# Part 2's first layer as Strassen's seven quarter products in place of eight

## The chip, the cores and the metric

The kernel runs on one core of one Trainium2 chip. The metric is the device time of one execution in microseconds, as the median of a few runs. The core has five engines that take their own instruction streams and wait for one another through semaphores: TensorE (PE, with its weight loads listed apart as PEld), VectorE (DVE), ScalarE (ACT), GpSimd (POOL) and SyncE (SP), which here only issues transfers.

## The reference

```python
scores = q @ mean_of_8(k).T / sqrt(64)          # per batch 8, head 8; 576 x 72
x = softmax(scores) @ mean_of_8(v)              # -> 4608 tokens x 512
h = max(x @ w1, x @ w2, x @ w3)                 # 512 -> 768
x = h @ w_out                                   # 768 -> 512
h = max(x @ moe2_w_in, 0)                       # 512 -> 2048   (first layer of part 2)
out = (h * h) @ moe2_w_out                      # 2048 -> 512   (second layer of part 2)
```

The feed-forward weights are 64-bit floats, which the kernel is handed as raw bits; q, k, v and the result (4608 x 512) are float32.

## The kernel before

Every product is done in three TensorE passes over values that are split into a high and a low part (`PARTS`: high x high, high x low, low x high); `split` makes the parts, the high one on ACT by a copy that rounds, the low one by a subtraction on DVE or POOL.

Part 1 works on 12 blocks of 384 tokens (`T1`). A block is 22 steps: 18 products of the max layer (L404, 12 matmuls of 384 columns each) and 4 of its output layer (L422, 18 matmuls each), whose results `ys` go to `y_dram` in DRAM by transfers on ACT's queue (L429). The attention of block j + 1 is woven between the steps of block j. So is, from block 2 to block 10, the preparation of part 2's weights: the 64-bit rows of `wi2` and `wo2` are loaded into a raw buffer (L118, two buffers for them in this stretch), turned into float32 by ACT and DVE (L133 to L138, result `wbits`), split in place (L115, L116, the low part on POOL), and stored to `wi2_dram` and `wo2_dram` (L386). `todo` is a list of pieces with due times, sorted once and emitted in that order. Behind it stands the planner of the framework, which emits on each engine the earliest piece in program order that it believes to be ready; a pool opened after others were closed takes their memory, and each of its tiles waits for the old tiles under it.

Part 2 works on 9 blocks of 512 tokens (`T2`). A block is 16 steps; in step f `moe2_in` multiplies a 128-column slice of the first layer's weights with the block (L505, 12 matmuls of 512 columns into one of three PSUM banks `ps`), ACT and DVE make the squared positive part and its two parts `g` (L511 to L515), and two steps later (`LAG`) `moe2_out` adds it into four PSUM banks `acc` (L526, 12 matmuls of 512 columns). All weights of part 2 stay in SBUF after they have been fetched once (L471): ten tiles of 512 KB during part 1's last block, 22 when part 1's memory comes free. `load_y` (L477) fetches and splits the next block's tokens.

SBUF from the bottom in part 1, by the pools' sizes per partition: `w_p` 96 KB (six `spare` tiles first, then 18 tiles of the max layer), `x_p` 24 KB, `h_p` 18 KB, `t_p` 6 KB (`hm`, then `ys`).

Of the kernel before, what the change touches and what calls it, by code (L numbers as in the profile page):

```python
# [10 lines left out]
F32 = mybir.dt.float32  # L11
F32R = mybir.dt.float32r
# [8 lines left out]
P = 128  # L21
# [5 lines left out]
DM = H * D  # L27
# [45 lines left out]
def as_f32(ap):  # L73
    return ap.bitcast(F32)
# [3 lines left out]
def attention_moe_kernel(ctx: ExitStack, tc: tile.TileContext, q, k, v, vn, w1, w2, w3, wo1, wi2, wo2, out):  # L78
# [18 lines left out]
    wi2_dram = [dram.tile([P, 2, 512], F32, name=f"wi2_dram{f}") for f in range(KF2)]  # L97
# [14 lines left out]

    def split(hl, src, engine=nc.vector):

        nc.scalar.activation(hl[:, 0], src, AF.Copy)  # L115
        engine.tensor_tensor(out=hl[:, 1], in0=src, in1=as_f32(hl[:, 0]), op=ALU.subtract)  # L116

    def load_raw(raw_pool, src):  # L118
# [4 lines left out]
    def convert(pool, raw_pool, raw, name, tag=None):  # L123

        low, high = raw[:, :, 0], raw[:, :, 1]
        a = raw_pool.tile([P, 512], I32, tag="row", name="wbits")
# [8 lines left out]
        if pool is None:  # L141
            w = raw.rearrange("p a b -> p (a b)").rearrange("p (c a) -> p c a", c=2).bitcast(F32R)
        else:
            w = pool.tile([P, 2, 512], F32R, name=name, tag=tag or name)
        split(w, as_f32(a), nc.gpsimd)
        return w
# [132 lines left out]

    def attend(j, b, s0, n, p, t):  # L280
# [4 lines left out]
        def load():  # L285
            if j == 0:
                kq = early([P, 2 * 512], "kq")
                kr.append(kq[:, :S])
                qr.append(kq[:, S : S + n])
                nc.sync.dma_start(out=kr[0], in_=k[b, p])  # L290
            elif first:
                kr.append(load_k(b, p))
            if j:
                qr.append(raw_p.tile([P, 512], F32, tag="row", name="qr")[:, :n])
# [10 lines left out]
        def softmax(tiles):  # L305
# [6 lines left out]
            ss = sm_p.tile([P, 3, 2, SP], F32, tag="ss", name="ss")[:m, :g]  # L312
# [66 lines left out]
    def load_w1(f, e):  # L379
        w1_t[f, e] = convert(w_p, raw_p, load_raw(raw_p, (w1, w2, w3)[e][f]), f"w1_{f}_{e}")  # L380

    def load_second(src, raw):
        raw.append(load_raw(raw_p, src))

    def prepare_second(raw, dst, name):
        nc.sync.dma_start(out=dst, in_=as_f32(convert(None, raw_p, raw.pop(), name)))  # L386

    def load_wo1(kk):
        wo1_t[kk] = convert(w_p, raw_p, load_raw(raw_p, wo1[kk]), f"wo1_{kk}", spare[kk])
        shared[0] = kk < KF1 - 1  # L390

    def moe1(j):
# [3 lines left out]
        for f in range(KF1):  # L396
# [19 lines left out]
            hs.append(h)  # L416
        for d in range(KD):
# [12 lines left out]
            yield  # L430
# [22 lines left out]
    for f in range(KF2):  # L453
        second += [(wi2[f], wi2_dram[f], f"wi2_{f}"), (wo2[f], wo2_dram[f], f"wo2_{f}")]
    for i, (src, dst, name) in enumerate(second):
        when, raw = STEPS * (SECOND[0] + (i + 0.5) * (SECOND[1] - SECOND[0]) / len(second)), []
        todo.append((when - LEAD_SECOND, functools.partial(load_second, src, raw)))
        todo.append((when, functools.partial(prepare_second, raw, dst, name)))
# [3 lines left out]

    y_p = ctx.enter_context(tc.tile_pool(name="y_p", bufs=1, side="right", reuse_waits="tile"))
    w2_p = ctx.enter_context(tc.tile_pool(name="w2_p", bufs=1, side="right", reuse_waits="tile"))
    wi2_t, wo2_t, y_t = {}, {}, {}
    NR = 10

    def fetch_second(t, f, pool):
        name, src = ("wi2", wi2_dram) if t is wi2_t else ("wo2", wo2_dram)
        t[f] = pool.tile([P, 2, 512], F32R, name=f"{name}s_{f}")  # L470
        nc.sync.dma_start(out=as_f32(t[f]), in_=src[f])  # L471


    order = sorted([(f, 0, wi2_t) for f in range(KF2)] + [(f + LAG, 1, wo2_t) for f in range(KF2)], key=lambda a: a[:2])
    loads = [(n, functools.partial(fetch_second, t, n - LAG if t is wo2_t else n)) for n, _, t in order]

    def load_y(j, d, pool):  # L477
        yr = y_p.tile([P, T2], F32, tag="yr", name="yr", bufs=2)
        t = 0
        while t < T2:  # L480
            i, o = divmod(j * T2 + t, T1)
            n = min(T2 - t, T1 - o)
            nc.sync.dma_start(out=yr[:, t : t + n], in_=y_dram[i][d, :, o : o + n])
            t += n
        y_t[j, d] = pool.tile([P, 2, T2], F32R, tag=f"y{d}", name=f"y{d}")
        split(y_t[j, d], yr)
# [7 lines left out]
    s1.close()  # L494
    w3_p = ctx.enter_context(tc.tile_pool(name="w3_p", bufs=1, reuse_waits="tile"))
    y2_p = ctx.enter_context(tc.tile_pool(name="y2_p", bufs=1, reuse_waits="tile"))
    g_p = ctx.enter_context(tc.tile_pool(name="g_p", bufs=3, reuse_waits="tile"))
    acc_ps = ctx.enter_context(tc.tile_pool(name="acc_ps", bufs=1, space=PSUM, reuse_waits="tile"))

    def moe2_in(j, f):  # L500
        ps = mm_ps.tile([P, T2], F32, tag="ps", name="ps")
        n = 0
        for kk in range(KD):
            for a, c in PARTS:
                nc.tensor.matmul(  # L505
                    ps, lhsT=wi2_t[f][:, a, kk * P : (kk + 1) * P], rhs=y_t[j, kk][:, c],
                    start=(n == 0), stop=(n == 3 * KD - 1),
                )
                n += 1
        r = g_p.tile([P, T2], F32, tag="r", name="r", bufs=2)  # L510
        nc.scalar.activation(r, ps, AF.Relu)  # L511
        g = g_p.tile([P, 2, T2], F32R, tag="g", name="g")
        nc.scalar.activation(g[:, 0], r, AF.Square)  # L513
        nc.vector.tensor_tensor(out=r, in0=r, in1=r, op=ALU.mult)  # L514
        nc.vector.tensor_tensor(out=g[:, 1], in0=r, in1=as_f32(g[:, 0]), op=ALU.subtract)  # L515
        return g

    NTT = T2 // P
    acc_t = {}

    def moe2_out(j, f, g):
        if f == 0:
            acc_t[j] = [acc_ps.tile([P, DM], F32, tag=f"acc{i}", name=f"acc{i}") for i in range(NTT)]
        for i in range(NTT):
            for n, (a, c) in enumerate(PARTS):
                nc.tensor.matmul(  # L526
                    acc_t[j][i], lhsT=g[:, a, i * P : (i + 1) * P], rhs=wo2_t[f][:, c],
                    start=(f == 0 and n == 0), stop=(f == KF2 - 1 and n == 2),
                )
            if f == KF2 - 1:  # L530
                o = g_p.tile([P, DM], F32, tag="o", name="o", bufs=4)
# [7 lines left out]
    late = [(n - AHEAD, functools.partial(f, w3_p)) for n, f in loads[NR:]]  # L539
    steps = [(j, f) for j in range(NB2) for f in range(KF2)]  # L540
    gs = {}
    for n, (j, f) in enumerate(steps):
        while late and late[0][0] <= n:
            late.pop(0)[1]()
        if f % 2 and f // 2 < KD and j + 1 < NB2:
            load_y(j + 1, f // 2, y2_p if j % 2 == 0 else y_p)
        gs[n] = moe2_in(j, f)
        if n >= LAG:
            moe2_out(*steps[n - LAG], gs.pop(n - LAG))
    for n in range(len(steps) - LAG, len(steps)):  # L550
        moe2_out(*steps[n], gs.pop(n))
# [41 lines left out]
```

## Time and profile before

| | |
|---|---|
| median of 3 runs | 1587.5 us (1587.31 to 1587.64) |
| profiled execution | 1590.31 us, span 1588.6 us |
| mean granted TensorE clock | 0.981 |
| PE busy | 1554.8 us (98%) |
| DVE, ACT, POOL busy | 748.9, 665.9, 174.1 us |
| HBM read, written | 83.89, 35.65 MB |

The span is the time from the first to the last instruction of the program; the profiled execution's own time lies 1.7 us above it. Matmul records overlap (one runs on while the next has begun), so the mean ns of one matmul is longer than the distance from one to the next; the latter is the length of a stretch over the matmuls in it.

### The profile page before, as it was taken

To read this page: it belongs to the slowest core of one execution; us is meant where nothing else is said; L and a number is where in the kernel's file an instruction comes from. 1 tells how busy PE (TensorE), PEld (TensorE's weight loads), DVE (VectorE), ACT (ScalarE), POOL (GpSimd) and SP (SyncE) were. 2 spreads that over 40 slices of the span, in tenths; PEclk is the share of its full clock that TensorE was granted. 3 is DMA by queue.
4 is the path that set the end of the run, shared out by engine and by line. 5 is a ranking of instruction groups with operands and counts; after the bars stand their busy time and mean duration, and the time that the engine had idled before them with its cause. 6 is when DMAs were issued, how large, how long until landed. Compare 5 with 4: busy or idle time off the path is not lost.

```text
span 1588.6 us, 21815 instructions
## 1 busy us (share of the span) xinstructions
PE 1554.8 (98%) x7994; PEld 1387.3 (87%) x7994; DVE 748.9 (47%) x1644; ACT 665.9 (42%) x1837; POOL 174.1 (11%) x223
## 2 busy tenths in 40 slices
PE   7889999999998999999999999999999999999998
PEld 5789999999998999999988888888888888888886
DVE  6896667675686657753233323232323223232222
ACT  7775556655566556653122223232322223232221
POOL 5541112222122102210000000000000000000000
PEclk7799999999999999999999999999999999999999
DMA  5552224432244214404270101010100001010000
GB/s 194 176 183 87 82 74 160 135 114 70 90 143 144 97 46 131 150 30 153 78 286 12 42 1 53 0 54 1 53 1 27 27 1 53 1 40 1 27 0 27
DMA packets 56652, 120.96 MB, mean 76 GB/s; under 512 B 6337, under 2 KB 29889, under 8 KB 56545
## 3 DMA queue, kind: packets, MB, share of 16 engines
q1 hardware_dynamic: 49632, 110.12, 20.8%
q10 hardware_dynamic: 6912, 9.44, 1.6%
q8 instruction: 63, 1.03, 0.3%
q14 instruction: 45, 0.36, 0.1%
HBM read 83.89 MB, written 35.65 MB: 75 GB/s over the span
## 4 chain that ended last, share of the span: by engine, by line
PE 89%; DMA 3%; DVE 3%; ACT 2%; issue 1%; POOL 1%; DVEq 0%; SPq 0%; ACTq 0%; POOLq 0%
PE ps L404 25%; PE ps L505 25%; PE acc L526 25%; PE ps L422 8%; PE sc L317 2%; PE tr L343 2%; PE av L369 1%; PE av L368 1%; DMA wraw<-in_w_dram 1%; DVE wbits L135 1%; ACT ss L322 1%; DMA wi_dram<-wraw 0%; DMA wraw<-in_wi_dram 0%; DVE wbits L138 0%; ACT wbits L133 0%
## 5 line engine op out<-in xcount | busy, mean ns | idle before, releaser
L404 PE MATMUL ps<-x,w 128*128 128x384 f32 x2592 | 505.6, 343 | 5.9 <-DVE hm L412 3.3
L404 PEld LDWEIGHTS ps<-x,w 128*128 128x128 f32 x2592 | 451.3, 191 | 9.5 <-DVE hm L412 4.1
L505 PE MATMUL ps<-y,wi2s 128*128 128x512 f32 x1728 | 420.6, 391 | 0.0
L526 PE MATMUL acc<-wo2s,g 128*128 128x512 f32 x1728 | 420.1, 391 | 0.0
L526 PEld LDWEIGHTS acc<-wo2s,g 128*128 128x128 f32 x1728 | 324.5, 188 | 71.5
L505 PEld LDWEIGHTS ps<-y,wi2s 128*128 128x128 f32 x1728 | 324.4, 188 | 71.5
L514 DVE TENSOR_TENSOR r<-r 128x512 f32<-128x512 f32 x144 | 99.5, 691 | 491.2 <-ACT g L513 491.2
L511 ACT ACTIVATE r<-ps 128x512 f32<-128x512 f32 x144 | 86.1, 598 | 546.6 <-PE ps L505 540.0
L422 PE MATMUL ps<-h,wo 128*128 128x384 f32 x864 | 166.8, 342 | 1.5 <-DVE hm L412 1.5
L422 PEld LDWEIGHTS ps<-h,wo 128*128 128x128 f32 x864 | 151.6, 191 | 1.7 <-DVE hm L412 1.7
L328 POOL TENSOR_TENSOR ss<-ss,st 128x144 f32<-128x144 f32 (+3 forms) x144 | 84.8, 589 | 438.7 <-DVE st L327 244.3
L412 DVE TENSOR_TENSOR hm<-ps,hm 128x384 f32<-128x384 f32 x144 | 79.5, 552 | 68.3 <-PE ps L404 63.1
L515 DVE TENSOR_TENSOR g<-r,g 128x512 fp32r<-128x512 f32 x144 | 99.5, 691 | 13.5 <-DVE r L514 0.9
L322 ACT ACTIVATE ss<-sc,st 128x72 f32<-128x72 f32 (+1 forms) x320 | 98.4, 314 | 12.4 <-DVE st L319 10.8
L345 ACT ACTIVATE pt<-tr 72x256 fp32r<-72x256 f32 (+1 forms) x160 | 56.4, 356 | 92.0 <-PE tr L343 90.0
L346 DVE TENSOR_TENSOR pt<-tr,pt 72x256 fp32r<-72x256 f32 (+1 forms) x160 | 62.0, 389 | 69.4 <-ACT pt L345 68.4
L513 ACT ACTIVATE g<-r 128x512 fp32r<-128x512 f32 x144 | 90.9, 632 | 4.3
L317 PE MATMUL sc<-kbd,qs 128*128 128x144 f32 (+1 forms) x480 | 79.1, 278 | 8.4 <-ACT kbd L177 5.5
L317 PEld LDWEIGHTS sc<-kbd,qs 128*128 128x128 f32 (+1 forms) x480 | 74.7, 197 | 12.5 <-issue 6.2
L343 PE MATMUL tr<-ident,ss 128*72 128x128 f32 (+1 forms) x320 | 60.5, 275 | 8.7 <-DVE pt L346 8.4
L322 ACT ACTIVATION_READ_ACCUMULATOR ss<-sc,st 128x1 f32 (+1 forms) x320 | 63.6, 199 | 0.0
L319 DVE TENSOR_REDUCE st<-sc 128x2 f32<-128x144 f32 (+3 forms) x144 | 45.4, 315 | 37.5 <-PE sc L317 37.0
(60 smaller groups left out, 1036.6 us busy)
## 6 DMA issues: line engine op xcount, KB each, us to landing
wraw<-in_wo_dram SPq DMA_DIRECT2D x22, 512.0 KB
wraw<-in_w_dram SPq DMA_DIRECT2D x18, 512.0 KB
y_dram<-ys ACTq DMA_DIRECT2D x48, 192.0 KB
out_dram<-o SPq DMA_DIRECT2D x36, 256.0 KB
wraw<-in_wi_dram SPq DMA_DIRECT2D x16, 512.0 KB
wi_dram<-wraw SPq DMA_DIRECT2D x16, 512.0 KB
wo_dram<-wraw SPq DMA_DIRECT2D x16, 512.0 KB
wi2s<-wi_dram SPq DMA_DIRECT2D x16, 512.0 KB
```

The source lines that it names most:

```text
L317: nc.tensor.matmul(src[:, i], lhsT=lhsT, rhs=kbd[:, p, l], start=(n == 0), stop=(n == 2))
L322: nc.scalar.activation(ss[:, i, h], src[:, i, h], AF.Exp, bias=st[:, 0, i, h : h + 1], accum_out=st[:, 1, i, h : h + 1],)
L328: nc.gpsimd.tensor_tensor(out=ss, in0=ss, in1=st[:, 2].rearrange("p g (h o) -> p g h o", o=1).to_broadcast([m, g, 2, SP]), op=ALU.mult,)
L343: nc.tensor.transpose(tr[:, h, :m], sms[c][:, h], ident[:m, :m])
L404: nc.tensor.matmul(ps, lhsT=w1_t[f, e][:, a, kk * P : (kk + 1) * P], rhs=x[kk][:, c], start=(n == 0), stop=(n == 3 * KD - 1),)
L422: nc.tensor.matmul(ps, lhsT=wo1_t[kk][:, a, d * P : (d + 1) * P], rhs=hs[kk][:, c], start=(n == 0), stop=(n == 3 * KF1 - 1),)
L505: nc.tensor.matmul(ps, lhsT=wi2_t[f][:, a, kk * P : (kk + 1) * P], rhs=y_t[j, kk][:, c], start=(n == 0), stop=(n == 3 * KD - 1),)
L511: nc.scalar.activation(r, ps, AF.Relu)
L513: nc.scalar.activation(g[:, 0], r, AF.Square)
L514: nc.vector.tensor_tensor(out=r, in0=r, in1=r, op=ALU.mult)
L515: nc.vector.tensor_tensor(out=g[:, 1], in0=r, in1=as_f32(g[:, 0]), op=ALU.subtract)
L526: nc.tensor.matmul(acc_t[j][i], lhsT=g[:, a, i * P : (i + 1) * P], rhs=wo2_t[f][:, c], start=(f == 0 and n == 0), stop=(f == KF2 - 1 and n ...
```

## The change

The first layer of part 2 takes two weight slices from each half of the hidden width and two halves (256 tokens, `HT`) of a block as a 2 x 2 by 2 x 2 product of quarters and does it in seven quarter products (the Winograd form of Strassen's scheme). A group (`gr`, four to a block) covers four slices of 128. `product` does two slices (u) of one of the seven products into one bank, in 2 x 6 matmuls of 256 columns. `moe2_in` adds the seven up on DVE. `mix_y` makes the four token combinations, `split_y` splits the seven operands. The weights' combinations are made in part 1 (`prepare_in`), per pair of rows: four stored tiles of 512, 512, 512 and 256 columns (`WIDTHS`). The first layer's weights stay in SBUF (14 KB per pair and partition, 8 pairs); the second layer's are fetched for every group of every block (`fetch_group`, four tiles of 512 KB, five buffers). `moe2_out` follows in the same group, in four phases of 12 matmuls of 512 columns. In part 1 the loads and conversions are tied by one-element copies on POOL to the latest `hm` of the max layer; `row` buffers go from four, shared with `qr`, to three and two of its own; three score tiles share an `ss` buffer.

```diff
+    def load_raw(raw_pool, src, after=None):
         raw = raw_pool.tile([P, 512, 2], I32, tag=place(0), name="wraw", bufs=1)
+        if after is not None:
+            nc.gpsimd.tensor_copy(as_f32(raw[:1, 0, :1]), after[:1, :1])
         nc.sync.dma_start(out=raw.rearrange("p a b -> p (a b)"), in_=src.bitcast(I32))
...
+    def prepare_in(raw, rows, f):
+        rows.append(convert(raw_p, raw[0], now[0]))
+        if f % 2 == 0:
+            split(in_place(raw[0]), rows[0], nc.gpsimd)
+            store_second(wi2_dram[f // 2][0], in_place(raw[0]))
+            return
...
+        combine(c[:, l], a2[:, l], a2[:, r], ALU.add)
+        combine(c[:, r], c[:, l], a1[:, l], ALU.subtract)
+        combine(a2[:, l], a1[:, l], a2[:, l], ALU.subtract)
+        combine(a1[:, r], a1[:, r], c[:, r], ALU.subtract)
+        split(in_place(raw[0]), a2, nc.gpsimd)
+        store_second(dst[1], in_place(raw[0]))
+        hi, lo = a2.bitcast(F32R), c.bitcast(F32R)
+        split_to(hi, lo, c, nc.gpsimd)
+        store_second(dst[2][:, 0], hi)
+        store_second(dst[2][:, 1], lo)
+        hi, lo = a1[:, l].bitcast(F32R), a1[:, r].bitcast(F32R)
+        split_to(hi, lo, a1[:, r], nc.gpsimd)
+        store_second(dst[3].rearrange("p a b -> p (a b)"), a1)
...
+    g_p = ctx.enter_context(tc.tile_pool(name="g_p", bufs=5, reuse_waits="tile"))
+    s_p = ctx.enter_context(tc.tile_pool(name="s_p", bufs=1, reuse_waits="tile"))
     w3_p = ctx.enter_context(tc.tile_pool(name="w3_p", bufs=1, reuse_waits="tile"))
+    wo_p = ctx.enter_context(tc.tile_pool(name="wo_p", bufs=5, reuse_waits="tile"))
...
+    def product(j, gr, m):
+        bank = mm_ps.tile([P, T2], F32, tag="ps", name="ps")
+        i, o = PLACES[m]
+        for u in range(2):
+            n = 0
+            for kk in range(2):
+                for a, c in PARTS:
+                    nc.tensor.matmul(
+                        bank[:, u * HT : (u + 1) * HT],
+                        lhsT=wi2_t[2 * gr + u][i][:, a, o + kk * P : o + (kk + 1) * P],
+                        rhs=y_t[j][m][:, c, kk], start=(n == 0), stop=(n == 5),
+                    )
+                    n += 1
+        return bank
+
+    def squared(c):
+        g = g_p.tile([P, 2, T2], F32R, tag="g", name="g")
+        nc.vector.scalar_tensor_tensor(out=c, in0=c, scalar=0.0, in1=c, op0=ALU.max, op1=ALU.mult)
+        split(g, c)
+        return g
+
+    def total(name, bank, other):
+        c = s_p.tile([P, T2], F32, tag=name, name=name)
+        nc.vector.tensor_tensor(out=c, in0=bank, in1=other, op=ALU.add)
+        return c
+
+    def moe2_in(j, gr):
+        m1 = product(j, gr, 1)
+        s1 = s_p.tile([P, T2], F32, tag="s1", name="s1")
+        nc.scalar.activation(s1, m1, AF.Copy)
+        s2 = total("s2", product(j, gr, 6), s1)
+        s3 = total("s3", product(j, gr, 7), s2)
+        m5 = product(j, gr, 5)
+        g = {(1, 1): squared(total("c0", m5, s3))}
+        nc.vector.tensor_tensor(out=s2, in0=m5, in1=s2, op=ALU.add)
+        g[0, 0] = squared(total("c1", product(j, gr, 2), s1))
+        g[1, 0] = squared(total("c0", product(j, gr, 4), s3))
+        g[0, 1] = squared(total("c1", product(j, gr, 3), s2))
+        return g
...
+    for p in range(1, NP2):
+        fetch_in(p, w3_p)
+        if p == 1:
+            fetch_group(0, 0)
+    for j in range(NB2):
+        for gr in range(NG):
+            if gr == 0 and j + 1 < NB2:
+                for r in range(2):
+                    load_y(j + 1, r)
+            g = moe2_in(j, gr)
+            if gr == NG - 2 and j + 1 < NB2:
+                mix_y(j + 1)
+            if gr == NG - 1 and j + 1 < NB2:
+                for m in ORDER:
+                    split_y(j + 1, m)
+            for h, half in ((1, 1), (0, 0), (1, 0), (0, 1)):
+                moe2_out(j, gr, h, half, g[h, half])
+            nxt = j * NG + gr + 1
+            if nxt < NB2 * NG:
+                fetch_group(*divmod(nxt, NG))
```

## Rows read from the trace of the kernel before

**Rows 1.** The page: busy us (share) x instructions of each engine.
```profile
PE 1554.8 (98%) x7994; PEld 1387.3 (87%) x7994; DVE 748.9 (47%) x1644; ACT 665.9 (42%) x1837; POOL 174.1 (11%) x223
```

**Rows 2.** Busy time by stage: us, each engine (instructions), clock, DMA share, GB/s.
```profile
140.00:300.00 160.00, 159.70 (x995) 157.38 (x994) 110.75 (x294) 93.79 (x312) 29.16 (x43) 1.00 0.32 102
...
450.00:600.00 150.00, 145.73 (x883) 142.22 (x883) 99.43 (x264) 87.70 (x289) 27.80 (x41) 0.98 0.30 101
...
788.00:1588.60 800.60, 795.11 (x3475) 651.70 (x3473) 231.61 (x338) 207.52 (x340) 0.00 (x0) 1.00 0.11 37
```

**Rows 3.** Groups of instructions: count | busy us, mean ns | idle before.
```profile
L505 PE MATMUL ps<-y,wi2s 128*128 128x512 f32 x1728 | 420.6, 391 | 0.0
L526 PE MATMUL acc<-wo2s,g 128*128 128x512 f32 x1728 | 420.1, 391 | 0.0
...
L505 PEld LDWEIGHTS ps<-y,wi2s 128*128 128x128 f32 x1728 | 324.4, 188 | 71.5
```

**Rows 4.** Windows of PE alone: 384-column stretch, then 512-column stretch.
```profile
745.00:785.00 40.00, 40.00 (x233) 1.00 0.27 100
...
1100.00:1500.00 400.00, 400.00 (x1749) 1.00 0.06 20
```

**Rows 5.** Timeline of PEld near 85 us: start, us, loads of 128 columns.
```profile
85.59 0.74 PEld L358 LDWEIGHTS av<-pt,vst 72*128 72x128 f32 x6
```

**Rows 6.** Groups of ACT, DVE, POOL by form: x count | busy us, mean ns.
```profile
L514 DVE TENSOR_TENSOR r<-r 128x512 f32<-128x512 f32 x144 | 99.5, 691 | 491.2 <-ACT g L513 491.2
L513 ACT ACTIVATE g<-r 128x512 fp32r<-128x512 f32 x144 | 90.9, 632 | 4.3
L533 DVE COPY o<-acc 128x512 f32<-128x512 f32 x18 | 12.3, 691 | 38.1 <-PE acc L526 37.5
L346 DVE TENSOR_TENSOR pt<-tr,pt 72x256 fp32r<-72x256 f32 x96 | 40.0, 416 | 46.2 <-ACT pt L345 45.5
L116 POOL TENSOR_TENSOR wraw<-wbits,wraw 128x512 fp32r<-128x512 f32 x32 | 41.2, 1287 | 61.6 <-ACT wraw L115 54.3 <-issue 3.8 <-DVE st L327 3.4
```

**Rows 7.** Timeline of DVE in a quiet part-2 step.
```profile
993.02 0.69 DVE L514 TENSOR_TENSOR r<-r 128x512 f32<-128x512 f32 x1 [3.98 <-ACT g L513]
993.81 0.69 DVE L515 TENSOR_TENSOR g<-r,g 128x512 fp32r<-128x512 f32 x1
```

**Rows 8.** Timeline where the next block's tokens are split.
```profile
960.15 0.69 DVE L514 TENSOR_TENSOR r<-r 128x512 f32<-128x512 f32 x1 [1.30 <-ACT g L513]
...
961.39 0.69 DVE L116 TENSOR_TENSOR y<-yr,y 128x512 fp32r<-128x512 f32 x1 [0.55 <-ACT y L115]
962.00 0.68 DVE L515 TENSOR_TENSOR g<-r,g 128x512 fp32r<-128x512 f32 x1
```

**Rows 9.** Timeline of the passage from part 1 to part 2.
```profile
788.57 0.32 SPq L471 DMA_DIRECT2D wi2s<-wi_dram  x1
...
790.98 8.55 PE L505 MATMUL ps<-y,wi2s 128*128 128x512 f32 x37
...
791.70 0.33 ACTq L429 DMA_DIRECT2D y_dram<-ys  x1
```

**Rows 10.** Windows around that passage, columns as in rows 2.
```profile
755.00:788.00 33.00, 33.00 (x192) 33.00 (x191) 7.13 (x13) 5.05 (x10) 0.00 (x0) 1.00 0.11 39
788.00:800.00 12.00, 12.00 (x59) 10.47 (x58) 4.06 (x6) 5.11 (x10) 0.00 (x0) 1.00 0.89 335
800.00:818.00 18.00, 18.00 (x80) 14.83 (x80) 5.86 (x9) 5.22 (x9) 0.00 (x0) 1.00 1.03 405
```

**Rows 11.** The chain that ended last, 485 to 492 us: start, us, what.
```profile
485.17 3.53 DMA wi_dram<-wraw
488.72 3.03 DMA wraw<-in_wi_dram
```

**Rows 12.** Windows behind it, columns as in rows 2.
```profile
494.00:506.00 12.00, 7.73 (x44) 6.33 (x43) 10.48 (x29) 9.07 (x34) 2.80 (x4) 0.90 0.44 145
506.00:513.00 7.00, 7.00 (x32) 6.83 (x32) 5.20 (x18) 4.63 (x15) 3.13 (x4) 0.68 0.27 104
```

More of the change, by code (lines that the diff above doesn't have):

```diff
@@ L95, in attention_moe_kernel @@
         )
-    wi2_dram = [dram.tile([P, 2, 512], F32, name=f"wi2_dram{f}") for f in range(KF2)]
+    wi2_dram = [[dram.tile([P, 2, n], F32, name=f"wi2_dram{f}_{i}") for i, n in enumerate(WIDTHS)] for f in range(KF2 // 2)]
     wo2_dram = [dram.tile([P, 2, 512], F32, name=f"wo2_dram{f}") for f in range(KF2)]
@@ L140, in convert, with in_place, weights @@
         )
[L141 to L145, printed above, removed]
+        return as_f32(a)
+    def in_place(raw):
+        return raw.rearrange("p a b -> p (a b)").rearrange("p (c a) -> p c a", c=2).bitcast(F32R)
+    def weights(pool, raw_pool, src, name, tag=None):
+        w = pool.tile([P, 2, 512], F32R, name=name, tag=tag or name)
+        split(w, convert(raw_pool, load_raw(raw_pool, src)), nc.gpsimd)
         return w
@@ L278, in attention, with scores @@
                 todo.append((at - pace + LAG_T + LAG_V, values))
+    used = []
+    def scores(g):
+        if not used or used[-1][1] + g > 3:
+            used.append([sm_p.tile([P, 3, 2, SP], F32, tag="ss", name="ss", bufs=3), 0])
+        used[-1][1] += g
+        return used[-1][0][:, used[-1][1] - g : used[-1][1]]
     def attend(j, b, s0, n, p, t):
@@ L293, in load @@
             if j:
-                qr.append(raw_p.tile([P, 512], F32, tag="row", name="qr")[:, :n])
+                qr.append(raw_p.tile([P, T1], F32, tag="qr", name="qr", bufs=2)[:, :n])
             nc.sync.dma_start(out=qr[0], in_=q[b, p, :, s0 : s0 + n])
@@ L416, in moe1 @@
             hs.append(h)
+            now[0] = hm
         for d in range(KD):
@@ L452, in attention_moe_kernel @@
     second = []
[L453 to L456, printed above, removed]
+    for f in range(0, KF2, 2):
+        rows = []
+        for i in (f, f + 1):
+            raw = []
+            second.append((wi2[i], raw, functools.partial(prepare_in, raw, rows, i)))
+        for i in (f, f + 1):
+            raw = []
+            second.append((wo2[i], raw, functools.partial(prepare_out, raw, i)))
@@ L464, in attention_moe_kernel @@
     w2_p = ctx.enter_context(tc.tile_pool(name="w2_p", bufs=1, side="right", reuse_waits="tile"))
[L465 to L486, printed above, removed]
@@ L488, in attention_moe_kernel, with fetch_in, fetch_out @@
-    early = [functools.partial(load_y, 0, d, y_p) for d in range(KD)]
-    early += [functools.partial(f, w2_p) for _, f in loads[:NR]]
+    wi2_t, wo2_t, yr_t, y_t = {}, {}, {}, {}
+    def fetch_in(p, pool):
+        wi2_t[p] = []
+        for i, n in enumerate(WIDTHS):
+            w = pool.tile([P, 2, n], F32R, name=f"wi2s_{p}_{i}")
+            nc.sync.dma_start(out=as_f32(w), in_=wi2_dram[p][i])
+            wi2_t[p].append(w)
+    def fetch_out(j, f):
+        wo2_t[j, f] = wo_p.tile([P, 2, 512], F32R, tag="wo2", name="wo2s")
+        nc.sync.dma_start(out=as_f32(wo2_t[j, f]), in_=wo2_dram[f])
@@ new lines, in load_y, with mix_y @@
+    def load_y(j, r):
+        yr = y_p.tile([P, 2, T2], F32, tag=f"yr{r}", name=f"yr{r}")
+        for i in range(2):
+            t = 0
+            while t < T2:
+                b, o = divmod(j * T2 + t, T1)
+                n = min(T2 - t, T1 - o)
+                nc.sync.dma_start(out=yr[:, i, t : t + n], in_=y_dram[b][2 * r + i, :, o : o + n])
+                t += n
+        yr_t[j, r] = yr
+    def mix_y(j):
+        (b11, b12), (b21, b22) = (
+            [yr_t[j, r][:, :, h * HT : (h + 1) * HT] for h in range(2)] for r in range(2)
+        )
+        src = {1: b11, 2: b21, 3: b22}
+        for m, a, b in ((5, b12, b11), (6, b22, 5), (7, b22, b12), (4, b21, 6)):
+            src[m] = y_p.tile([P, 2, HT], F32, tag=f"t{m}", name=f"t{m}")
+            nc.vector.tensor_tensor(out=src[m], in0=a, in1=src[b] if isinstance(b, int) else b, op=ALU.subtract)
+        y_t[j] = src
@@ L490, in attention_moe_kernel, with split_y @@
+    def split_y(j, m):
+        y = y_p.tile([P, 2, 2, HT], F32R, tag=f"y{m}", name=f"y{m}")
+        split(y, y_t[j][m])
+        y_t[j][m] = y
+    ORDER = (1, 6, 7, 5, 2, 4, 3)
+    early = [functools.partial(load_y, 0, r) for r in range(2)] + [functools.partial(mix_y, 0)]
+    early.append(functools.partial(fetch_in, 0, w2_p))
+    early += [functools.partial(split_y, 0, m) for m in ORDER]
     for i, f in enumerate(early):
@@ L498, in attention_moe_kernel @@
     acc_ps = ctx.enter_context(tc.tile_pool(name="acc_ps", bufs=1, space=PSUM, reuse_waits="tile"))
[L500 to L511, printed above, removed]
+    def product(j, gr, m):
[9 more added lines that the diff above has]
+                        rhs=y_t[j][m][:, c, kk], start=(n == 0), stop=(n == 5),
+                    )
+                    n += 1
+        return bank
@@ new lines, in attention_moe_kernel, with moe2_out @@
+    acc_t = {}
+    def moe2_out(j, gr, h, half, g):
+        if j not in acc_t:
+            acc_t[j] = [acc_ps.tile([P, DM], F32, tag=f"acc{i}", name=f"acc{i}") for i in range(T2 // P)]
+        first, last = gr == 0 and h == (1 if half else 0), gr == NG - 1 and h == (0 if half else 1)
+        for n, (a, c) in enumerate(PARTS):
+            for u in range(2):
+                for i in range(2):
+                    nc.tensor.matmul(
+                        acc_t[j][2 * half + i],
+                        lhsT=g[:, a, u * HT + i * P : u * HT + (i + 1) * P],
+                        rhs=wo2_t[j, 4 * gr + 2 * u + h][:, c],
+                        start=(first and n == 0 and u == 0), stop=(last and n == 2 and u == 1),
+                    )
+        if last:
+            for i in range(2 * half, 2 * half + 2):
+                o = y_p.tile([P, DM], F32, tag=f"t{4 + i}", name="o")
@@ L536, in moe2_out, with fetch_group @@
                 nc.sync.dma_start(out=out[j * T2 + i * P : j * T2 + (i + 1) * P], in_=o)
[L539 to L551, printed above, removed]
+    def fetch_group(j, gr):
+        for h in (1, 0):
+            for u in range(2):
+                fetch_out(j, 4 * gr + 2 * u + h)
+    for p in range(1, NP2):
[18 more added lines that the diff above has]
+                fetch_group(*divmod(nxt, NG))
 def kernel(**inputs):
```

62 lines of the change are left out of this document (31 added, 31 removed).

## The prediction

> **What bounds the kernel now.** The page comes first: PE is busy 98% of the span, and no other engine half of it [rows 1]. The windows by stage say where PE is not full: after the first 140 us almost nowhere, 4.3 us in one stretch around 500 us, and part 2, the last 800 us, has none missing apart from the tail behind its last matmul, with DVE and ACT under 30% [rows 2]. The groups confirm it for the lines that change: neither L505 nor L526 shows idle time before it [rows 3]. So part 2 costs what its matmuls cost one after the other, and whatever else is done there counts only if it makes PE wait. Since matmul records overlap, the price of one is read from windows: 400 us over 1749 matmuls is 228.7 ns for one of 512 columns, 40 us over 233 is 171.7 ns for one of 384 [rows 4].
>
> **The matmuls of the first layer.** Before: 9 blocks x 16 steps x 12 = 1728 of 512 columns, 1728 x 228.7 = 395.2 us. After: 9 x 4 groups x 7 products x 12 = 3024 of 256 columns. The columns fall to 7/8, but the number of matmuls and weight loads grows by 3/4, so the price of a 256-column matmul decides. The trace before has no long run of them. The line through the two prices of [rows 4] falls by 0.445 ns a column and gives 114.7 at 256. If instead one column takes one period of the granted 2.4 GHz (0.417 ns; the clock column of both windows is 1.00), the 512 row gives 122.0 and the 384 row 118.4. Below it lies a floor by the weight loads: near 85 us six loads of 128 columns span 0.74 us; with the last record about 0.19 long, as those of L505 are, that is five distances of 110 ns [rows 3, 5]. A 256-column matmul therefore still outlasts its neighbour's weight load, though by only some ten ns. The price cannot be over the 384 one, 171.7, unless small matmuls get dearer. Bounds 110 and 172; I take 120, between the two clock figures, and 114 to 123 as the likely spread. 3024 x 120 = 362.9 us: **32.3 us less** (23 to 50 less over the likely spread). Break-even is 395.2 / 3024 = 130.7 ns.
>
> The Trainium skill, page "TensorE: Matmul & The Clock Gate", section "Back-to-back issue gap", gives the isolated distance as N/2.4 + 2.5 ns, thus about 216 at 512 and 109 at 256. By it the layer would save 1728 x 215.8 - 3024 x 109.2 = 43 us. The 512 row shows 13 ns more than that rule, and a fixed cost per matmul is paid 1296 times more often here, so the trace speaks against the larger gain.
>
> **The second layer's matmuls** are the same 1728 of 512 columns, in another order: 0.
>
> **DVE and ACT in part 2.** Per group DVE gets 15 operations of 512 columns: s2, s3, the second use of m5, and for each of the four results a sum, a square and a low part. By [rows 6] such an operation is 0.69 us from SBUF (L514) and from PSUM (L533), and 0.79 us from one to the next that depends on it [rows 7]; 15 x 0.79 = 11.9 us. A group on PE is 84 x 0.12 + 48 x 0.229 = 10.1 + 11.0 = 21.1 us. Per block come four sums and seven splits more, 11 x 0.69 = 7.6 us in 84. So DVE is filled to some 65% and hides. ACT has five copies a group, near 0.63 each [rows 6], and hides too.
>
> Latency is the tighter question. Products take 12 x 0.12 = 1.44 us each and rotate through three banks; the fourth (m5) and the seventh (m3) share one. m5 ends at 5.8 us, m3 wants the bank at 8.6. The bank is free after both DVE readings of m5. If DVE takes the second reading before or within the first split's wait on ACT, that is about 6.0 + 0.79 + 0.69 + 0.7 = 8.2 us: in time, with 0.4 us to spare. The source has it behind the whole split; then it ends at 6.0 + 0.79 + 0.69 + 0.71 (ACT) + 0.72 + 0.7 = 9.6, and PE waits 1.1 us in each of 36 groups, 40 us. The planner decides. In [rows 8] it put the low part of the next block's tokens between L514 and L515 of one step, which the source keeps together, so it does fill DVE's waits with what is ready: I take 0. The last results need no care: the four output phases of 2.75 us start at 10.1, 12.8, 15.6 and 18.3, and even a strict order has the four `g` done at 9.6, 12.6, 15.5 and 18.4, where a phase wants the low part only in its last third. Handing over 396 banks or phases instead of 288 costs nothing visible before (no idle, [rows 3]); I add 1 us, between 0 and 4.
>
> **Weights on their way in.** In steady state a group fetches 2.1 MB in 21.1 us, 100 GB/s, against 405 seen with the queues full [rows 10]; five buffers let the tiles come half a group ahead. The start is another matter. The order on SP is pair 1, the four output tiles of group 0, pairs 2 to 7, the next block's tokens, then the output tiles of group 1. The fourth output tile lies 140 to 144 KB up (`g_p` 20, `s_p` 10, `w3_p` 98, then 12), where `t_p` held `ys`, whose last store is issued at 791.70 [rows 9]: about 794 with its landing. Before, too, SP stood in order behind the first tile that was not free (L471 starts at 788.57 though tiles above it were free, [rows 9], and the transfers idle at 39 GB/s from 755 to 788, [rows 10]). From 794 on: 0.5 MB, pairs 2 to 7 with 11.0, tokens 2.1, two tiles 1.0, together 14.7 MB, at 405 GB/s 36 us, so 830. PE wants these two tiles at 791.1 + 21.1 + 10.1 = 822.3. That is 8 us late, once. The planner may move products of group 2 into the hole (up to four before banks and `g` buffers run out, 5.8 us), so I put 6 us idle, between 0 and 11 (335 GB/s). Idle PE has a second price: after the 4.3 us missing between 494 and 506 the clock is at 0.68 over the next 7 us, that is mostly at the 1.2 GHz level [rows 12]; some 7 us at half speed cost up to 3.4. **Sum +9**, bounds 0 and 14. Group 0 itself is served: its first two tiles are there by 796, wanted at 801.
>
> **Part 1.** Each of 8 pairs adds four half-width DVE operations (256 columns, 0.42 by L346 in [rows 6]: 1.7 us), two splits of 512 and one of 256 for one of 512 (1.3 + 0.7 us POOL more, about 1 us ACT), four more store transfers of 0.8 MB, and one-element POOL copies, of which there are 64. Over the 500 us they run in, DVE goes from about 68% [rows 2] by 13 us more, POOL by some 20: PE covers it. The risk is order. POOL now waits for a raw buffer to be stored where SP alone did, and behind it on POOL stand the softmax products; and the raw buffer of an odd row is held longer. What that does the trace shows once: a store of 3.5 us and the load behind it of 3.0 [rows 11] came late, ACT stood at the conversion, and the softmax behind it cost PE 4.3 us and the clock 3.4 [rows 12]. The change may remove this one (-8) or bring one or two more (+8, +16). I take **+2**. The tail is as before: two evictions side by side behind the last matmul.
>
> **Sum.** -32.3 + 1 + 9 + 2 = -20.3. Against the profiled execution's 1590.3 that gives 1570.0; that execution is 2.8 above the median, and none of the terms lies in that difference, so **1567** for the median.
>
> **Rivals.**
> *The loads come early enough* (chance 0.22): if the planner sends pairs 2 to 5, whose memory is free before 780, ahead of the tiles that wait for 794, the idle queue of [rows 10] takes them and the +9 goes: 1558. Against it: SP's standing at 788.57.
> *Part 1 stumbles more* (0.15): two further stretches like the one at 500 us, +16: 1583.
> *A bank too late* (0.08), the other side: the second reading of m5 behind the split, +40: 1607. It decides from the point where that reading ends later than 8.6 us into the group; more than half of the gain is gone at 0.5 us per group.
> *Small matmuls do not follow the line* (0.10), the change then not doing what it says: at 131 ns the seven products cost what the eight did, and 12 us of losses stay: 1599. For it: only ten ns lie between stream and weight load. Against it: in [rows 5] loads keep 110 ns under a narrower stream.
>
> **How the numbers follow.** The forecast keeps 0.45: 1567, own range 1558 to 1577. A difference under 0.2%, 3.2 us, cannot be told from none. Faster by more: 0.45 + 0.22, most of the stumbling case and a sliver of the fourth, 0.81. The same: 0.06. Slower: the bank case, nearly all of the fourth, 0.13. The range 1554 to 1584 takes in the first three cases with their spreads and leaves the last two out.
>
> **What would show it.** Windows in part 2: distance of the 256-column matmuls 114 to 123 ns (over 130: the main step is wrong). Idle before the product line by line: none within groups (1 us on DVE in each group: the bank case). Between 800 and 840 us: one idle stretch of 2 to 11 us before the second group's output matmuls, released by a transfer, with the clock column below 1.00 behind it. Part 1's end within some us of 791. It would go wrong most by the price of a small matmul, since each 3.3 ns there are 10 us.

## The result and the profile after

The changed kernel takes 1546.3 us (median of 4 runs, 1545.93 to 1548.26) against 1587.57: the ratio is 0.9739, 95% interval 0.9724 to 0.9754. The forecast was 1567, its range 1554 to 1584: right in direction, but 41.3 us came instead of 20, and the time lies below the range.

The page of the changed kernel, engines and the groups that answer to [rows 1, 3]:

```profile
PE 1509.4 (98%) x9290; PEld 1416.2 (92%) x9290; DVE 947.7 (61%) x1991; ACT 623.0 (40%) x1772; POOL 200.2 (13%) x303
...
L645 PE MATMUL acc<-wo2s,g 128*128 128x512 f32 x1728 | 412.6, 391 | 0.0
...
L600 PE MATMUL ps<-y,wi2s 128*128 128x256 f32 x3024 | 376.8, 280 | 3.4 <-DVE s L629 2.9
```

PE is as full as before, so the time went where the matmuls became shorter, and 3.4 us of waiting are all that the 252 products found. The windows by stage (columns as in [rows 2]):

```profile
126.00:488.00 362.00, 361.83 (x2249) 357.14 (x2248) 253.55 (x680) 217.33 (x722) 81.99 (x145) 1.00 0.36 116
488.00:553.00 65.00, 62.90 (x377) 61.74 (x376) 47.89 (x120) 39.87 (x125) 12.83 (x26) 0.97 0.38 118
...
783.50:1539.70 756.20, 752.77 (x4753) 680.59 (x4751) 408.99 (x641) 154.22 (x254) 0.00 (x0) 1.00 0.38 136
```

Of the 756.2 us of part 2's matmuls, 1728 x 228.7 ns = 395.2 us are the second layer's at the price of [rows 4]; the other 361.0 over 3024 is 119.4 ns for one of 256 columns, waits included. The stages of part 1 can be cut where the last output-layer matmul of each block starts. In the two profiled executions (us):

| | first block ends | blocks 1 to 6 | block 7 | blocks 8 to 10 | block 11 | part 2 |
|---|---|---|---|---|---|---|
| before | 131.7 | 359.7 | 70.7 | 178.8 | 49.9 | 797.8 |
| changed | 126.1 | 361.6 | 65.0 | 180.7 | 49.9 | 760.9 |

So 36.9 us came from part 2 and 7.5 from part 1, 44.4 between two profiled executions whose medians differ by 41.3.

The hole forecast for the second group's output matmuls is not there. PE's timeline around it:

```profile
783.49 11.36 PE L600 MATMUL ps<-y,wi2s 128*128 128x256 f32 x90
...
798.55 10.62 PE L645 MATMUL acc<-wo2s,g 128*128 128x512 f32 x46
809.00 20.66 PE L600 MATMUL ps<-y,wi2s 128*128 128x256 f32 x174
829.50 11.53 PE L645 MATMUL acc<-wo2s,g 128*128 128x512 f32 x50
```

and SP's issues (start, us until the last of the row was issued):

```profile
737.94 5.98 SPq L557 DMA_DIRECT2D yr<-y_dram  x8
744.33 42.42 SPq L542 DMA_DIRECT2D wi2s<-wi_dram  x9
786.85 2.74 SPq L547 DMA_DIRECT2D wo2s<-wo_dram  x4
789.64 20.54 SPq L542 DMA_DIRECT2D wi2s<-wi_dram  x19
811.14 4.87 SPq L547 DMA_DIRECT2D wo2s<-wo_dram  x5
```

The second group's output tiles are issued at 811 to 816, behind all first-layer weights, as foreseen. But the next block's tokens had gone at 738, five first-layer tiles beyond pair 1 stand before 787, and the planner ran 174 products in one go before it turned to the outputs at 829.5. 54 of them finish group 1; the other 120 are ten whole products, the seven of group 2 and three of group 3.

### The profile page after: what moved, and what is told of

Read it like the earlier page. It is cut to its first block, busy times and chain, and to the rows that moved or that the text cites. A ratio compares the mean times of both kernels' runs of the same rounds, so it can differ in the third digit from the quotient of the medians.

```text
span 1544.2 us, 25098 instructions
## 1 busy us (share of the span) xinstructions
PE 1509.4 (98%) x9290; PEld 1416.2 (92%) x9290; DVE 947.7 (61%) x1991; ACT 623.0 (40%) x1772; POOL 200.2 (13%) x303
## 4 chain that ended last, share of the span: by engine, by line
PE 88%; DVE 4%; DMA 3%; ACT 2%; issue 1%; SPq 0%; POOL 0%; DVEq 0%; ACTq 0%; POOLq 0%
PE ps L465 26%; PE acc L645 25%; PE ps L600 21%; PE ps L484 9%; PE sc L344 2%; PE tr L370 2%; DMA out_dram<-o 2%; PE av L396 1%; PE av L395 1%; ACT ss L349 1%; DVE wbits L153 0%; DMA kq<-in_q_dram 0%; ACT wraw L149 0%; DVE hm L473 0%; DVE wbits L150 0%
## 5 line engine op out<-in xcount | busy, mean ns | idle before, releaser
L645 PE MATMUL acc<-wo2s,g 128*128 128x512 f32 x1728 | 412.6, 391 | 0.0
L600 PEld LDWEIGHTS ps<-y,wi2s 128*128 128x128 f32 x3024 | 370.4, 188 | 13.1 <-PE ps L600 4.0
L600 PE MATMUL ps<-y,wi2s 128*128 128x256 f32 x3024 | 376.8, 280 | 3.4 <-DVE s L629 2.9
L645 PEld LDWEIGHTS acc<-wo2s,g 128*128 128x128 f32 x1728 | 316.4, 188 | 62.5
L121 ACT ACTIVATE g<-c 128x512 fp32r<-128x512 f32 x144 | 90.8, 631 | 410.9 <-DVE c L611 403.9
L617 DVE TENSOR_TENSOR s<-ps,s 128x512 f32<-128x512 f32 x72 | 49.8, 691 | 262.4 <-PE ps L600 261.8
L617 DVE TENSOR_TENSOR c<-ps,s 128x512 f32<-128x512 f32 x144 | 98.8, 686 | 24.9 <-PE ps L600 21.7
L355 POOL TENSOR_TENSOR ss<-ss,st 128x144 f32<-128x144 f32 (+3 forms) x144 | 73.2, 510 | 309.4 <-DVE st L354 237.8
L122 DVE TENSOR_TENSOR g<-c,g 128x512 fp32r<-128x512 f32 x144 | 98.6, 685 | 17.4 <-ACT g L121 16.5
L611 DVE SCALAR_TENSOR_TENSOR c<-c 128x512 f32<-128x512 f32 x144 | 98.8, 687 | 2.1
```

Source lines behind the costliest of these rows:

```text
L121: nc.scalar.activation(hi, src, AF.Copy)
L122: engine.tensor_tensor(out=lo, in0=src, in1=as_f32(hi), op=ALU.subtract)
L600: nc.tensor.matmul(bank[:, u * HT : (u + 1) * HT], lhsT=wi2_t[2 * gr + u][i][:, a, o + kk * P : o + (kk + 1) * P], rhs=y_t[j][m][:, c, kk] ...
L611: nc.vector.scalar_tensor_tensor(out=c, in0=c, scalar=0.0, in1=c, op0=ALU.max, op1=ALU.mult)
L617: nc.vector.tensor_tensor(out=c, in0=bank, in1=other, op=ALU.add)
L645: nc.tensor.matmul(acc_t[j][2 * half + i], lhsT=g[:, a, u * HT + i * P : u * HT + (i + 1) * P], rhs=wo2_t[j, 4 * gr + 2 * u + h][:, c], st ...
```

## The experiments

All times are medians of 4 to 7 runs, except for e6 and e9, which have one run each; beside these runs the kernel before took 1586.4 to 1587.7. The stages of the table above (us), for the profiles of all runs but e6:

| | first block ends | 1 to 6 | 7 | 8 to 10 | part 2 | median |
|---|---|---|---|---|---|---|
| e1 before + buffers | 130.1 | 382.3 | 60.2 | 178.8 | 798.1 | 1598.98 |
| e2 changed, no ties | 131.4 | 393.0 | 60.0 | 178.8 | 762.1 | 1577.7 |
| e3 changed, old buffers | 127.1 | 358.6 | 67.5 | 178.6 | 761.2 | 1546.33 |
| e4 group 2 in order | 126.9 | 361.2 | 65.0 | 181.3 | 771.6 | 1558.77 |
| e5 m5 behind the split | 126.3 | 361.5 | 64.1 | 180.6 | 763.4 | 1548.69 |
| e7 before + ties | 126.2 | 359.8 | 67.4 | 178.5 | 797.7 | 1582.45 |
| e8 no preparation in 7 | 126.8 | 366.4 | 59.8 | 179.1 | 761.4 | 1542.29 |
| e9 before again | 130.2 | 359.2 | 71.2 | 178.7 | 797.8 | 1588.72 |
| e10 changed again | 125.4 | 361.2 | 66.2 | 180.4 | 764.1 | 1548.42 |
| e11 as e8 | 125.9 | 365.0 | 59.7 | 179.1 | 760.4 | 1541.55 |
| e12 none in 4 and 7 | 126.0 | 372.6 | 59.8 | 178.9 | 760.8 | 1550.68 |

**Was the hole filled, or never there?** e4 pins one matmul behind what stands before it in the source.

```diff
-                    n += 1
+                    n += 1 if (j, gr, m, u, n) != (0, 2, 1, 0, 0) else len([tc.keep_in_program_order(ins)])
```

> The changed kernel with one edge more: the first matmul of the third group of the first block may not be issued before the second group's output phases, so the planner can't put that group's products ahead. Nothing of part 1 moves. Theory (the output weights of the second group are late as forecast, and the planner fills the hole with the next group's products): PE idle of 5 to 12 us appears between 810 and 830 us, released by a transfer, with the granted clock down behind it; median 1553 to 1562. Rival (the weights are there in time and the order is chance): 1546 within 2 us, no idle over 1 us.

It took 1558.77 us, 12.5 more: the theory, with the idle time at the lower edge of what it gave. PE's timeline, and windows with the columns of [rows 2]:

```profile
809.95 6.53 PE L600 MATMUL ps<-y,wi2s 128*128 128x256 f32 x54
821.42 13.85 PE L645 MATMUL acc<-wo2s,g 128*128 128x512 f32 x48 [4.95 <-DMA wo2s<-wo_dram]
```

```profile
816.00:822.00 6.00, 1.05 (x7) 0.77 (x5) 4.74 (x8) 1.67 (x3) 0.00 (x0) 0.83 1.03 406
822.00:830.00 8.00, 8.00 (x26) 5.96 (x25) 0.00 (x0) 0.00 (x0) 0.00 (x0) 0.70 0.30 119
```

Without the products put ahead, PE stands 4.95 us until a transfer lands, and the clock is lower around and behind it (0.83, then 0.70 in the mean). The 48 output matmuls behind the wait come (13.85 - 0.39) / 47 = 286 ns apart instead of 228.7, which is 2.7 us. So the hole cost 7.7 us of the 10.7 by which part 2 is longer; 2.5 more are waits for DVE elsewhere in part 2, which the unchanged kernel also shows in another execution (e10, below). The lateness of the forecast was real, 5 us where 8 were worked out. In the changed kernel the planner filled the hole.

**The bank that comes too late.** e5 pins DVE's second reading of m5 to its place in the source.

```diff
-        nc.vector.tensor_tensor(out=s2, in0=m5, in1=s2, op=ALU.add)
+        tc.keep_in_program_order(nc.vector.tensor_tensor(out=s2, in0=m5, in1=s2, op=ALU.add))
```

> The changed kernel with DVE's second reading of the fourth product (m5) pinned behind the first result's whole split, as the source has it. Theory A (the rival of the prediction, a bank too late): the seventh product finds its bank taken and PE waits 1 to 1.7 us in each of 36 groups, 36 to 60 us in all; median 1582 to 1606. Theory B (as at the start of part 2, the planner fills such a hole, here with output matmuls of the same group): under 5 us in all, median 1546 to 1551, and between the sixth and the seventh product the trace shows output matmuls.

1548.69 us, 0.3 to 2.4 more than the changed kernel's two medians. That is the time of theory B, but not its mechanism. In the changed kernel DVE reads m5 twice in a row (L617, then L629), before the square:

```profile
894.61 0.69 DVE L617 TENSOR_TENSOR c<-ps,s 128x512 f32<-128x512 f32 x1 [0.72 <-PE ps L600]
895.22 0.68 DVE L629 TENSOR_TENSOR s<-ps,s 128x512 f32<-128x512 f32 x1
895.82 0.68 DVE L611 SCALAR_TENSOR_TENSOR c<-c 128x512 f32<-128x512 f32 x1
```

In e5 the second reading starts 3.35 us behind the first instead of 0.61, after the reading of the fifth product (m2, at 895.55):

```profile
894.13 0.69 DVE L617 TENSOR_TENSOR c<-ps,s 128x512 f32<-128x512 f32 x1 [0.72 <-PE ps L600]
...
895.55 0.69 DVE L617 TENSOR_TENSOR c<-ps,s 128x512 f32<-128x512 f32 x1
...
897.48 0.69 DVE L629 TENSOR_TENSOR s<-ps,s 128x512 f32<-128x512 f32 x1
...
899.88 0.69 DVE L617 TENSOR_TENSOR c<-ps,s 128x512 f32<-128x512 f32 x1
```

PE's timeline there:

```profile
890.63 7.70 PE L600 MATMUL ps<-y,wi2s 128*128 128x256 f32 x64
898.17 4.72 PE L645 MATMUL acc<-wo2s,g 128*128 128x512 f32 x20
902.73 0.87 PE L600 MATMUL ps<-y,wi2s 128*128 128x256 f32 x6
```

The 64 matmuls run to the end of the group: its fourth sum, which needs the seventh product, starts at 899.88, before any further product. So the last twelve of them are the seventh product, and it starts at about 896.8 (890.63 + 52 x 0.118), before the second reading of m5 has begun. It cannot sit in m5's bank. Of the three banks only that of the fifth product is free then, read out at 896.24. The same holds in 35 of the 36 groups: the seventh product starts 0.7 to 2.8 us before the second reading. So the banks are not handed out in strict turn, and the collision behind the 40 us did not arise. What a seventh product would cost that really had to wait for m5's bank, no run shows.

**The price of a matmul.** e6 narrows ten of twelve matmuls, by block, and so leaves out part of the first layer's sums.

> The changed kernel with ten of every twelve matmuls of a product cut to fewer columns (the first of each six keeps 256, the rest of the columns are left out): 256, 240, 224, 208, 192, 160, 128, 64, 256 in blocks 0 to 8. It leaves out part of the sums; the time asked is the distance of the matmuls. Theory (stream price down to a floor by the weight loads): 118 at 256, 111 at 240, then 108 to 111 at every smaller width. Rival (a price per column plus a constant all the way): 104 at 224, 91 at 192, 64 at 128.

PE's timeline, the longest run of one block each, at 240, 224, 192, 160 and 128 columns (a row also counts the 256-column matmuls among them and ten of the next block's width):

```profile
931.82 9.50 PE L602 MATMUL ps<-y,wi2s 128*128 128x240 f32 x83
...
1014.52 9.49 PE L602 MATMUL ps<-y,wi2s 128*128 128x224 f32 x83
...
1179.96 9.45 PE L602 MATMUL ps<-y,wi2s 128*128 128x192 f32 x83
...
1262.58 9.44 PE L602 MATMUL ps<-y,wi2s 128*128 128x160 f32 x83
...
1345.36 9.43 PE L602 MATMUL ps<-y,wi2s 128*128 128x128 f32 x83
```

Less the last record (about 0.25 us), over 82 distances: 112 to 113 ns at each of these widths, at a granted clock of 1.00. The rival's 104 and 91 did not come; the theory's floor did, 1 to 2 ns higher than expected. The 174 matmuls of the changed kernel above give (20.66 - 0.28) / 173 = 117.8 at 256. So there is a floor at 112, and the change stands 6 ns over it: with fewer columns a matmul would have saved these 6 ns at most. That the weight loads set the floor shows where loads have fewer columns, in the changed kernel's attention:

```profile
65.17 0.59 PEld L344 LDWEIGHTS sc<-kbd,qs 128*96 128x96 f32 x6
```

Less the last record of 0.16 us these six come 86 ns apart, before matmuls of 144 columns, while loads of 128 columns keep 112 in e6 even before matmuls of 128: the distance goes with the columns of the load. The Trainium skill, page "TensorE: Matmul & The Clock Gate", section "LDWEIGHTS (loading the stationary operand)", gives the time of a load in ns as its columns / 1.2, whatever the rows, an estimate of 107 ns for 128 columns; the trace agrees within 5 ns.

**Part 1's gain.** One theory lays it to the buffer edits, the other to the ties; e1 gives the buffer edits to the kernel before, e3 takes them from the changed one, e2 takes the ties.

```diff
-        a = raw_pool.tile([P, 512], I32, tag="row", name="wbits")
+        a = raw_pool.tile([P, 512], I32, tag="row", name="wbits", bufs=3)
...
-                qr.append(raw_p.tile([P, 512], F32, tag="row", name="qr")[:, :n])
+                qr.append(raw_p.tile([P, T1], F32, tag="qr", name="qr", bufs=2)[:, :n])
...
-            ss = sm_p.tile([P, 3, 2, SP], F32, tag="ss", name="ss")[:m, :g]
+            ss = scores(g)[:m]
```

> The kernel before with only the buffer edits of part 1: conversion rows in three buffers, query rows in two of their own, three score tiles to one ss buffer. Theory (these edits shorten the start-up of part 1): its first block ends near 126 us where the kernel before has 131.7, and the median falls by 4 to 6 us to about 1582. Rival (the start-up differs because the planner orders everything anew, or from run to run): the first block ends within 1.5 us of 131.7 and the median stays within 3 us of 1587.5.

> The changed kernel with the buffers of part 1 as before: four row buffers shared by conversions and queries, an ss buffer for every score tile. Theory (the buffer edits shorten the start-up): first block ends near 131 us instead of 126.1, median 1550 to 1552. Rival (they don't): first block within 1.5 us of 126, median 1546 within 2 us.

```diff
-        raw.append(load_raw(raw_p, src, now[0]))
+        raw.append(load_raw(raw_p, src))
...
-        rows.append(convert(raw_p, raw[0], now[0]))
+        rows.append(convert(raw_p, raw[0]))
```

> The changed kernel without the one-element POOL copies that tie the loads and conversions of part 2's weights to the max layer. Theory (the ties keep the conversions from standing in the way and so removed most of the stretch at 500 us): without them such stretches come back, 5 to 16 us in all, median 1551 to 1562, with PE idle between 126 and 733 us of 5 us or more where the changed kernel has 3.5. Rival (the ties do nothing for the time): 1546 within 2 us.

The buffer theory fell on both sides: the kernel before with the new buffers is 0.8% slower (1598.98, ratio 1.0079, interval 1.0064 to 1.0094), which neither theory nor rival of e1 expected, and the changed one with the old buffers is the same (1546.33). Without ties it takes 1577.7, about 31 us more, twice the most that was expected. The windows of two stretches of part 1, first of e2, then of the changed kernel:

```profile
131.40:403.40 272.00, 253.37 (x1491) 243.40 (x1490) 207.08 (x506) 177.02 (x543) 84.53 (x99) 0.97 0.56 190
403.40:763.20 359.80, 359.80 (x2241) 355.85 (x2240) 209.99 (x596) 182.50 (x638) 33.17 (x75) 1.00 0.14 43
```

```profile
126.10:366.50 240.40, 240.40 (x1490) 237.63 (x1489) 165.06 (x444) 141.73 (x469) 50.99 (x92) 1.00 0.36 114
366.50:733.40 366.90, 363.38 (x2242) 357.77 (x2241) 250.96 (x659) 219.27 (x711) 84.66 (x147) 1.00 0.34 111
```

The same four blocks of PE work take 272.0 us instead of 240.4, with DVE at 76% where it had 69%. What is added there shows in the count of conversions (by the line that shifts `wbits`), per 122 us from the time at the head of the column:

| conversions from | 118 | 240 | 362 | 484 | 606 |
|---|---|---|---|---|---|
| before | 3 | 9 | 7 | 5 | 8 |
| e1 before + buffers | 18 | 14 | 0 | 0 | 0 |
| e2 changed, no ties | 16 | 14 | 2 | 0 | 0 |
| changed | 4 | 7 | 7 | 7 | 7 |
| e3 changed, old buffers | 3 | 8 | 7 | 7 | 7 |

With the new buffers and no ties (e1, e2) the planner runs nearly all conversions before 362 us, about the middle of part 1. In the kernel before, the old buffers held them back, unevenly; in the changed one the ties do it, whatever the buffers (e3). Which of the buffer edits lets them go early was not tested by itself; the likely one is the row buffers that the conversions no longer share with the queries.

e7 gives the ties alone to the kernel before, e9 looks at that kernel once more.

```diff
-        raw.append(load_raw(raw_p, src))
+        raw.append(load_raw(raw_p, src, now[0]))
```

> The kernel before with one thing from the change: the one-element POOL copies that tie the loads and conversions of part 2's weights to the max layer. Theory (the ties spread the conversions evenly and are worth what part 1 gained beyond the start-up): the longest block is under 68 us where the kernel before has 70.7, median 1582 to 1586. Rival (the shared row buffers already hold the conversions back in the kernel before, so the ties add nothing): 1587 within 1.5 us.

> The kernel before, unchanged, to see whether its late k load in block 0 belongs to the kernel or to one execution. Theory (two loads of part 2's weights, due early, stand before the k load in the queue): DVE again waits for that load near 122 us, PE is idle there for about a microsecond, and the first block ends between 129 and 132 us. Rival (chance of one execution): the first block ends near 126 us.

The ties alone are worth 5.3 us (1582.45 against 1587.73, ratio 0.9967, 0.9956 to 0.9977), small but clear of 1: the theory. The first block ends at 126.2 as in the changed kernel, which had not been expected of it, and block 7 shrinks to 67.4. e9 says why the first block is longer without them. Its issues on SP:

```profile
118.24 0.33 SPq L120 DMA_DIRECT2D wraw<-in_wi_dram  x1
118.90 0.33 SPq L193 DMA_DIRECT2D kr<-in_k_dram  x1
```

and DVE's wait behind them, first in e9, then in e7, where no load of part 2's weights is issued in the first block:

```profile
123.85 0.75 DVE L203 TENSOR_REDUCE ks<-kr 128x72 f32<-128x576 f32 x1 [2.04 <-DMA kr<-in_k_dram]
```

```profile
118.19 0.33 SPq L197 DMA_DIRECT2D kr<-in_k_dram  x1
...
121.09 0.75 DVE L207 TENSOR_REDUCE ks<-kr 128x72 f32<-128x576 f32 x1 [0.80 <-DMA kr<-in_k_dram]
```

A 512 KB weight load that is due only near the end of the next block stands before a k load that DVE waits for: from the k load's issue to DVE's use of it are 4.95 us in e9 and 2.90 in e7. It came again in e9, so it belongs to the kernel, though how much the clock adds at the start differs from one execution to the next.

**A faster version.** Block 7 keeps its long stretch in the changed kernel. e8 and e11 (one kernel) keep the preparation out of it, e12 out of block 4 too; e10 is the changed kernel beside them.

```diff
-        when = STEPS * (SECOND[0] + (i + 0.5) * (SECOND[1] - SECOND[0]) / len(second))
+        when = STEPS * (SECOND[0] + (i + 0.5) * (SECOND[1] - 1 - SECOND[0]) / len(second))
+        when += STEPS if when >= 7 * STEPS else 0
```

> The changed kernel with the loads and conversions of part 2's weights kept out of block 7 (due times over eight blocks, those from block 7 on moved by one block). Theory (the stretch near 495 us comes from conversions that stand among the attention's work): block 7 takes about 60.5 us instead of 65.0, median 1541 to 1543. Rival (the attention alone makes that stretch): block 7 stays near 65, median 1546 within 1.5 us.

> The changed kernel, unchanged, beside the next two on one chip: 1546 within 1.5 us, first block's end near 126 us, block 7 about 65 us.

> The changed kernel with the weights' preparation kept out of block 7, once more beside the unchanged one. Its profile showed the long stretch moved from block 7 (59.8 us) to block 4 (65.9 us), so theory: no gain, 1546 within 1.5 us. Rival: the 4 us of its earlier median are real, 1542 within 1.5 us.

> The changed kernel with the preparation kept out of blocks 4 and 7. Theory (both long stretches come from preparation in these two blocks): no block between 1 and 9 over 62 us, median 1541 to 1543. Rival (the stretch moves on to another block or the denser preparation costs as much): 1546 within 2 us.

e8 took 1542.29 us, as its theory said. e11 took 1541.55 (ratio to before 0.9708, interval 0.9693 to 0.9723), e10 1548.42 (0.9744, 0.9727 to 0.9761), which is 0.9 us outside its expectation. No run of e8 or e11 (1540.48 to 1545.21) is as long as any of the changed kernel (1545.62 to 1548.89), so this version is faster than both kernels, though only by 0.3 to 0.4% than the changed one. The theory of e11, no gain, fell, and so did that of e12: there block 7 is short again, but blocks 4 to 6 take 191.6 us instead of 181.3, and the median is 1550.68, also over the rival's 1548.

Preparation is part of the long block 7: it takes 60 us wherever no conversion or only one falls into it (e1, e2, e8, e11, e12) and 65 to 71 with four. It is not the whole cause of such a stretch: in e8 and e11 block 4 is the long one (65.8 and 64.4 us) with four conversions, in e12 it holds one and takes 65.3, and other blocks with four take 60. What sets it off stays open.

e11's part 1 is 3.1 us shorter than that of e10, its part 2 3.7 us, though the edit doesn't touch part 2. There the difference is PE's wait for DVE's second reading of m5 (us in total, times, longest), first in e10, then in e11:

```profile
PE ps L600 <- DVE s L629: 5.9, 6, 1.6
```

```profile
PE ps L601 <- DVE s L630: 2.3, 5, 0.5
```

The same wait is 2.9 us in the first profile of the changed kernel, whose part 2 is 3.2 us shorter than in e10. So two executions of one kernel differ there by as much as e10 and e11 do, and at most the 3.1 us of part 1 can be put to the edit (1.3 from the profile of e8 to the first one of the changed kernel). Why the wait differs between executions is not shown.

## Why the prediction was wrong

**The first layer** was right: 119.4 ns for a 256-column matmul where 120 was taken, 34.2 us (395.2 - 361.0) where 32.3 stood. The floor by the weight loads is there too, at 112 where 110 stood (e6), and a 256-column matmul stays above it. The larger gain of 43 us did not come: at 0.417 ns a column the 117.8 ns leave 11 ns of fixed price a matmul, near the 15 that the 228.7 ns of the 512-column row leave.

**DVE and the banks**: right that almost nothing waits (3.4 us in all), with the second reading directly behind the first, as hoped. The premise that the fourth and the seventh product share a bank is wrong as a rule: in e5, where the second reading comes late, the seventh takes another bank, so the rival's 40 us do not follow from a late reading. DVE is busy 409.0 of the 756.2 us, 54% where some 65% stood.

**Weights on their way in (+9)** is the step that failed first. With the order forced (e4) the hole is there and costs 7.7 us, 4.95 of them idle, so lateness and price were sized about right; in the changed kernel it cost nothing. What failed is the count of the work that could fill it: the step allowed the planner "up to four" products before banks and `g` buffers run out, and it found ten. DVE's timeline shows where they wait:

```profile
824.68 0.69 DVE L122 TENSOR_TENSOR g<-c,g 128x512 fp32r<-128x512 f32 x1 [0.16 <-ACT g L121]
...
833.12 0.69 DVE L122 TENSOR_TENSOR g<-c,g 128x512 fp32r<-128x512 f32 x1 [2.07 <-ACT g L121]
...
835.18 1.41 DVE L617 TENSOR_TENSOR s<-ps,s 128x512 f32<-128x512 f32 x2
```

At 824.68 the last free `g` buffer is filled; the next one comes at 833.12, behind the first output matmuls. In between one result each stays in `c0` and `c1`, the first product of the following group in `s1`, and three more products in their banks, two of which are read at 835.18. And the tokens of the next block did not queue with the weights: their transfers went at 738, 49 us before the first output tiles.

**Part 1 (+2)** is the step that failed next, in sign. It counted the ties as 64 small POOL copies and saw in the order they impose only a risk for the softmax, not that they hold the loads and conversions back. They are worth 31 us in the changed kernel, whose buffers would otherwise let the conversions crowd (e2), and 5.3 us in the kernel before (e7), where two weight loads leave block 0 and the rest is spread evenly. The forecast named a gain of 8 as possible, if the one stretch of [rows 11, 12] went away, but took a loss; the stretch shrank (block 7 from 70.7 us to 65.0). In the profiles part 1 gave 7.5 us.

**The remainder**: the forecast was -20.3. With 0 for the +9, -5 to -7.5 for the +2, and -34.2 for -32.3 + 1, it is -39 to -42, which takes in the measured -41.3. The tail and the second layer's matmuls, which leave some 2 us of room, were not followed up. The rival "the loads come early enough" named the right absence for a reason that held only for some of the tiles.

## What to carry to other kernels

Where a planner orders the instructions by readiness, a late transfer costs only what it can't fill with later work: list all work that is ready and every place where a result can wait, not the next few pieces in the source. Before a held bank is given a price, see from the trace which bank the next product takes. Ask of every buffer and every dependency of background work when it lets that work start, because giving it more room can pull it forward into the way of the critical stage (e1, e2), and a tie of one element can be worth far more than it costs. And for a matmul made narrower, find the distance of the weight loads first: it was the floor here.

## What the runs showed of the hardware

Matmuls of 240 to 128 columns all come 112 to 113 ns apart in e6, where each brings its own 128-column weights. In the stretch of e6 with 64 columns in ten of twelve, the granted clock is 0.76, a mean between the levels of 2.4 and 1.2 GHz, though PE's records show no idle time in this window (one run; columns as in [rows 2]):

```profile
1375.00:1455.00 80.00, 80.00 (x401) 72.98 (x402) 36.92 (x58) 13.57 (x23) 0.00 (x0) 0.76 0.21 80
```

DVE operations of 0.69 us that do not depend on one another start 0.61 us apart (894.61, 895.22, 895.82 above), against 0.79 for a dependent pair in [rows 7]; the 11.9 us a group that the prediction charged to DVE at 0.79 each were too many.
